# H3 convolution beside a SiLU feed-forward, on one core: where rows and signals are transposed, how the norm's root is made, and the list's DMA prices

## The chip, the core and the metric

One core of a Trainium2 chip. The metric is the device time of one execution in microseconds; of a set of runs the median counts. All traces are of the core's hardware profiler, one execution each.

## The reference

All inputs are float32; S = 2048 rows, D = 1024 channels, F = 3584.

```python
xn = layernorm(q)                       # per row, (x - m) / sqrt(v + 1e-5)
k_shift = causal_conv(k, shift_k)       # 4 taps per channel
kv = k_shift * v
y = irfft(rfft(kv, 2S) * rfft(ssm_k, 2S))[:S] + kv * ssm_D     # per channel
out = q + xn * y + silu(xn @ w1) @ w2
```

## The kernel before

**Number format.** Every product of float32 quantities runs as three float16 products: each factor is split into a high and a low part (`split`, line 363: one ScalarE activation for the high part, one VectorE instruction, line 345, for the rest), and high x high, high x low and low x high are accumulated. Lines 947 to 949 are those three products of the first feed-forward matmul, 1075 to 1077 of the second, 1506 to 1508 of the convolution's forward transform and 1697 to 1699 of its inverse.

**Feed-forward.** The first matmul treats its rows in two halves of 1024 (index `sp` 0 and 1), and within a half it uses a Strassen scheme with seven products (`PRODUCTS`): the factors of x are A11, A12, A21, A22 (upper and lower four row blocks, left and right half of the channels) and the sums S1 to S4 of them; the factors of w1 are B11 to B22 and T1 to T4. For the first half the x factors stay in SBUF in the places `x0` to `x7`. For the second half the sums are made row by row (`more_sums`), split and stored to DRAM (`xsp`), and read back by a transposing DMA (`load_x`, one DMA of 1 MB for each of seven factors) as soon as the first half's last use of a place is over.

**Norm and first factors, before.** `load_row` loads a row block (128 rows) as `xt`. `ln_rows` takes statistics on VectorE (`bn_stats`, line 493, two halves; `bn_aggr`, then two small copies, lines 498 and 499), in groups of 2, 2, 4 and 8 blocks; for each group ScalarE makes the square root, VectorE the reciprocal and one Newton step (lines 507 to 512), and VectorE normalizes each block in place (line 522). `ON_ACT` and `APPLY` name blocks whose statistics or normalization run on ScalarE; both are empty. `transposes` (line 539) turns the eight blocks of the first half with TensorE, each half block as four 128x128 float32 transposes into one of three PSUM tiles `ft`. From the transposed tiles the factors are split; `keep` copies the transposed upper blocks back over their rows with ScalarE, `lower_sums` copies A21 to `s` with ScalarE, and the sums S1 to S4 are made of transposed tiles on VectorE.

**The convolution.** Eight channel groups of 128 (index g). `gate` makes `acc` (the shifted k times v) with rows on partitions of its own order; `signal_parts` scales and splits it into `cm` (one buffer, `CMB` = 1), and two transposing DMAs, issued by SP (`X`, line 335), bring the high and low parts to `hi` and `lo`; the filter's parts are split into the same tiles. `stage1` multiplies them with the DFT constants `cfw` into PSUM tiles `ps`: each of four tiles t of a group has two banks, each first with three products, then evacuated by ScalarE (`to_spec`: `diff`), then with three more, then evacuated again. `PSB` is the number of `ps` banks, 3, and `py`, for the norms and the inverse transform, has 4 - `PSB`. While the second feed-forward matmul runs, a `ps` or `py` tile may use a bank of the feed-forward's ring `ff` where more than one is free (`spare`). `forward`, `product` and `inverse` are VectorE work on `spec` and `tmp`.

**Order.** All this is recorded by generators (streams), and a list scheduler, `Order.run`, writes the instructions of all engines in one order. Each operation has an engine, a busy time, a delay and a margin; DMAs have bytes besides, which pass through one modelled pipe (`self.pipe`). The stream whose head can start first, less its bias, goes next. The engines' queues then run in this order as they stand, so a price that is off shows as a wait at the head of a queue. Prices of DMAs: `L` for plain ones from SP (0.4 us busy), `X` for transposing ones (0.6 us busy, 1.2 times the bytes), `G` for accumulating ones from GpSimd (bytes as they are). The pipe is

```python
self.pipe = max(self.pipe, t + 3.0) + op.nbytes / 330e3
```

A table load is priced where an activation's function (Sqrt or Silu) is not the last one that was loaded.

Of the kernel before, what the change touches and what calls it, by code (L numbers as in the profile page):

```python
# [11 lines left out]
F32 = mybir.dt.float32  # L12
BF16 = mybir.dt.bfloat16
F16 = mybir.dt.float16
I32 = mybir.dt.int32
# [22 lines left out]
PSB = 3  # L38
XGB = 4
CMB = 1  # L40
ON_ACT = ()
APPLY = ()
# [69 lines left out]
class Order:  # L112
# [58 lines left out]
    def run(self):  # L171
        while self.streams:
# [122 lines left out]
def h3_ffn_kernel(ctx, tc, x, kp, vs, fs, shift, dskip, w1, w2, cfwd, cinv, out):  # L295
# [36 lines left out]
    def X(o, i, m=0.3):  # L332

        n = size(o) * o.shape[0] * mybir.dt.size(o.dtype)
        return Op("SP", 0.6, 0.1, lambda: nc.sync.dma_start(o, i, transpose=True), [i], [o], m, 1.2 * n)
# [12 lines left out]
    def a_act(o, i, func, scale=1.0, bias=None, total=None):  # L348
# [7 lines left out]
        p.table = func if func in (AF.Sqrt, AF.Silu) else None  # L356
# [23 lines left out]
    mean = cst.tile([P, NT], F32, name="mean")  # L380
# [38 lines left out]
    sums_r = s1_r = xst_r = Halves(order, lnp, "s", 6)  # L419
# [48 lines left out]
    def load_row(t):  # L468
        yield xts_r.ready
        xts[t] = xns[t] = xts_r.tile([P, D], uses=6 if t < 4 else 2)  # L470
# [3 lines left out]
    def ln_rows():  # L474
        for t0, n, bias in ((0, 2, 0.26), (2, 2, 0.17), (4, 4, 0.15), (8, 8, 0.03)):
            yield bias
            q = slice(t0, t0 + n)
            mv = lnp.tile([P, 6, 8], F32, name="mv", bufs=2)
            m = mv[:, :, 0:n]
            order_in = (8, 9, 12, 13, 10, 11, 14, 15) if n == 8 else range(t0, t0 + n)  # L480
            for n_, t in enumerate(order_in):
                yield flag["xt", t]
                xt, i = xts[t][0], slice(t - t0, t - t0 + 1)
                if t in ON_ACT:
                    yield a_act(wide, xt, AF.Copy, total=m[:, 1, i])
                    yield a_act(m[:, 0, i], m[:, 1, i], AF.Copy, -1.0 / D)
                    yield a_act(wide, xt, AF.Square, 1.0, m[:, 0, i], total=m[:, 1, i])
                    yield a_act(m[:, 3, i], m[:, 1, i], AF.Copy, 1.0 / D)
                    continue
                st = lnp.tile([P, 2, 6], F32, name="st", bufs=2)  # L490
                ag = lnp.tile([P, 2], F32, name="ag", bufs=2)
                for a in range(2):
                    yield V(lambda: nc.vector.bn_stats(st[:, a, :], xt[:, a * W:(a + 1) * W]), st[:, a, :],
                            [xt[:, a * W:(a + 1) * W]], us=0.65)

                def moments():
                    nc.vector.bn_aggr(ag, st)
                    nc.vector.tensor_scalar(m[:, 0, i], ag[:, 0:1], -1.0, None, op0=MUL)
                    nc.vector.tensor_copy(m[:, 3, i], ag[:, 1:2])
                p = V(moments, m[:, 0, i], [st], us=0.5)  # L500
                p.writes.append(m[:, 3, i])
                yield p
            yield V(lambda: nc.vector.tensor_scalar(m[:, 3, :], m[:, 3, :], 1e-5, None, op0=ADD), m[:, 3, :], [m[:, 3, :]], us=0.15)
            yield a_act(m[:, 4, :], m[:, 3, :], AF.Sqrt)

            def chain(m=m, q=q):
                nc.vector.reciprocal(m[:, 4, :], m[:, 4, :])
                nc.vector.tensor_mul(m[:, 5, :], m[:, 4, :], m[:, 4, :])
                nc.vector.tensor_mul(m[:, 5, :], m[:, 5, :], m[:, 3, :])
                nc.vector.tensor_scalar(m[:, 5, :], m[:, 5, :], -0.5, 1.5, op0=MUL, op1=ADD)  # L510
                nc.vector.tensor_mul(rstd[:, q], m[:, 4, :], m[:, 5, :])
                nc.vector.tensor_mul(nmr[:, q], m[:, 0, :], rstd[:, q])
            p = V(chain, rstd[:, q], [m[:, 3, :], m[:, 4, :], m[:, 0, :]], us=1.05)
            p.writes += [nmr[:, q], m[:, 5, :]]
            yield p
            for t in order_in:
                xt, i = xts[t][0], slice(t - t0, t - t0 + 1)
                if t in APPLY:
# [3 lines left out]
                yield V(lambda: nc.vector.tensor_scalar(xt, xt, m[:, 0, i], rstd[:, t:t + 1], op0=ADD, op1=MUL),  # L522
                        xt, [xt, m[:, 0, i], rstd[:, t:t + 1]], us=0.78)
                flag["xn", t].set()

    pts = []

    def transposes():
        jobs = [(t, a) for t in range(4) for a in range(2)]
        jobs += [(4 + i, a) for i in range(4) for a in range(2)]  # L530
        for t, a in jobs:
            yield flag["xn", t]
            xn, tok = xns[t]
            yield ft.ready
            pt, ptok = ft.tile([P, KH, P], uses=2)

            def mm():
                for c in range(KH):
                    nc.tensor.transpose(pt[:, c, :], xn[:, (KH * a + c) * P:(KH * a + c + 1) * P], ident)
            yield T(mm, pt, [xn], 0.5, m=0.3)  # L540
            tok.set()
            pts.append((pt, ptok))

    def next_pt():
        return bool(pts)

    def first_rows():
        for n, name in enumerate(("A11", "A12")):
            xo[0][name], xtok[0][name] = places[XPLACE[name]].tile([P, 4, KH, 2, P], F16)
        for t in range(4):  # L550
# [1275 lines left out]
```

## Time and profile before

| | before |
|---|---|
| median of 3 runs | 1296.15 us (1293.06 to 1300.64) |
| profiled execution, device time | 1294.81 us |
| its span in the trace | 1293.0 us |
| mean granted TensorE clock | 0.987 |
| busy: TensorE, VectorE, ScalarE, GpSimd | 1235.7, 1147.6, 727.0, 133.1 us |
| DMA moved | 289.25 MB, mean 224 GB/s |

The device time of the profiled execution holds 1.8 us besides the span. TensorE's busy time counts each matmul with its latency, so that neighbours overlap; its pace is read from the starts. In rows of groups, the columns are line, engine, operation, output and inputs by the program's names, shapes and count, then busy us and mean ns of one, then idle us just before them and what ended it. Stages are read as windows of the span.

### The profile page before, as it was taken

The page shows a single profiled execution, that of the slowest core. Times are in us where ns is not written, and L with a number is a line of the kernel's source. Part 1 is how long each engine was busy: PE and PEld are TensorE (multiplying, and loading weights), DVE is VectorE, ACT ScalarE, POOL GpSimd, SP SyncE. Part 2 cuts the span into 40 slices and gives each one's busy share as a digit, 9 for nine tenths or more (in the row PEclk, how much of TensorE's full clock was granted, in tenths as well). Part 3 has the DMA queues.
Part 4 walks back from the last instruction along what each step waited for, and adds up shares of the span by engine and source line. Part 5 has one row for each costly group of instructions (what it writes and reads, how often), then busy time and mean ns, then how long its engine had stood idle before and what let it go on. Part 6 is the DMA issues. An engine that isn't in the chain of part 4 may idle for free.

```text
span 1293.0 us, 16973 instructions
## 1 busy us (share of the span) xinstructions
PE 1235.7 (96%) x5954; PEld 590.2 (46%) x5954; DVE 1147.6 (89%) x1525; ACT 727.0 (56%) x1153; POOL 133.1 (10%) x141
## 2 busy tenths in 40 slices
PE   6899999998999999988999999999989999999997
PEld 6444444443444454434544444444444454444453
DVE  7999998896569989989998989999999989999961
ACT  6857886775676688656754442454173263542321
POOL 0000000000000020000310120120030030123241
PEclk9899999999999999999999999999999999999999
DMA  9447888899899999879997597599587597979785
GB/s 325 153 157 228 288 302 299 290 262 226 215 352 337 322 282 352 254 197 269 259 318 163 99 243 163 94 241 304 136 168 195 131 186 211 253 145 151 159 144 77
DMA packets 281364, 289.25 MB, mean 224 GB/s; under 512 B 78400, under 2 KB 197184, under 8 KB 280000
## 3 DMA queue, kind: packets, MB, share of 16 engines
q1 hardware_dynamic: 254544, 263.27, 67.5%
q0 software_dynamic: 26736, 24.92, 15.4%
q8 instruction: 46, 0.75, 0.3%
q14 instruction: 38, 0.31, 0.1%
HBM read 184.05 MB, written 96.73 MB: 217 GB/s over the span
## 4 chain that ended last, share of the span: by engine, by line
PE 35%; DVE 29%; DMA 16%; issue 12%; ACT 4%; POOL 2%; SPq 1%; POOLq 0%; ACTq 0%; DVEq 0%
DVE spec L342 8%; PE ff L948 6%; PE ff L947 6%; PE ff L949 6%; PE ff L1075 4%; PE ff L1077 4%; PE ff L1076 4%; DVE tmp L342 3%; DMA wraw<-in_w 3%; DMA lo<-cm 3%; DVE x L345 2%; POOL out L339 2%; DVE ht L345 2%; DVE wo L345 2%; DVE acc L345 2%
## 5 line engine op out<-in xcount | busy, mean ns | idle before, releaser
L1075 PE MATMUL ff<-x,wo 128*128 128x512 f16 x864 | 327.4, 379 | 5.1 <-DMA hi<-in_vs 2.7
L1077 PE MATMUL ff<-x,wo 128*128 128x512 f16 x864 | 327.4, 379 | 0.0
L1076 PE MATMUL ff<-x,wo 128*128 128x512 f16 x864 | 327.4, 379 | 0.0
L947 PE MATMUL ff<-x,wo 128*128 128x512 f16 (+1 forms) x808 | 306.2, 379 | 14.7 <-ACT hf L353 5.8
L948 PE MATMUL ff<-x,wo 128*128 128x512 f16 (+1 forms) x808 | 306.2, 379 | 2.6 <-DVE x L345 2.6
L949 PE MATMUL ff<-x,wo 128*128 128x512 f16 (+1 forms) x808 | 306.4, 379 | 1.8 <-DVE wo L345 1.8
L342 DVE TENSOR_TENSOR spec<-spec 128x512 f32<-128x512 f32 (+2 forms) x256 | 261.0, 1052 | 2.2
L1076 PEld LDWEIGHTS <-wo 128*128 128x128 f16 x864 | 84.5, 98 | 104.4 <-issue 6.2
L1077 PEld LDWEIGHTS <-wo 128*128 128x128 f16 x864 | 84.5, 98 | 102.0
L1075 PEld LDWEIGHTS <-wo 128*128 128x128 f16 x864 | 85.4, 99 | 98.6
L948 PEld LDWEIGHTS <-wo 128*128 128x128 f16 x808 | 79.8, 99 | 105.7 <-issue 18.5
L949 PEld LDWEIGHTS <-wo 128*128 128x128 f16 x808 | 79.7, 99 | 99.8 <-issue 6.4
L947 PEld LDWEIGHTS <-wo 128*128 128x128 f16 x808 | 81.4, 101 | 93.8 <-issue 3.0
L353 ACT ACTIVATE hf<-ff,invc 128x512 f32<-128x512 f32 x64 | 43.5, 680 | 102.6 <-PE ff L1077 93.0
L339 POOL DMA_DIRECT2D out<-hf x63 | 55.8, 886 | 437.9 <-ACT hf L353 390.5
L342 DVE TENSOR_TENSOR tmp<-spec 128x2048 f32<-128x2048 f32 (+1 forms) x48 | 92.1, 1932 | 0.7
L345 DVE SCALAR_TENSOR_TENSOR ht<-hf,wsc,ht 128x1024 f16<-128x1024 f32 (+1 forms) x56 | 67.3, 1203 | 18.0 <-ACT ht L353 17.9
L339 POOL DMA_DIRECT2D out<-xg x40 | 45.2, 1284 | 300.2 <-DMA lo<-cm 136.3
L345 DVE SCALAR_TENSOR_TENSOR wo<-raw,wsc,wo 128x512 f16<-128x512 f32 (+1 forms) x56 | 55.9, 1012 | 17.1 <-ACT wo L353 17.1
L353 ACT ACTIVATE ht<-hf,wsc 128x1024 f16<-128x1024 f32 (+1 forms) x56 | 60.7, 1085 | 15.5 <-DMA hs<-ht 5.0
L345 DVE SCALAR_TENSOR_TENSOR acc<-kin,taps,acc 128x1024 f32<-128x1024 f32 x48 | 61.4, 1278 | 8.8 <-ACT acc L353 8.8
L353 ACT ACTIVATE spec<-spec 128x1024 bf16<-128x1024 f32 x32 | 33.7, 1052 | 51.6 <-DVE spec L342 51.6
(178 smaller groups left out, 1747.5 us busy)
## 6 DMA issues: line engine op xcount, KB each, us to landing
wo<-hs SPq DMA_DIRECT2D x160, 256.0 KB, 3.7
hs<-ht SPq DMA_DIRECT2D x80, 256.0 KB, 5.6
out<-hf POOLq DMA_DIRECT2D x63, 256.0 KB, 4.4
raw<-in_w SPq DMA_DIRECT2D x28, 512.0 KB, 5.6
wraw<-in_w SPq DMA_DIRECT2D x24, 512.0 KB, 6.6
w2n<-in_w SPq DMA_DIRECT2D x24, 512.0 KB, 6.6
kin<-in_kp SPq DMA_DIRECT2D x16, 704.0 KB, 5.4
xt<-in_x SPq DMA_DIRECT2D x16, 512.0 KB, 7.3
```

The costliest lines, as they stand in the source:

```text
L339: return Op("POOL", 1.1, 3.0, lambda: nc.gpsimd.dma_start(o, i, accum_op=ADD), [i], [o], m, n)
L342: return V(lambda: nc.vector.tensor_tensor(o, a, b, op=op), o, [a, b], **k)
L345: return V(lambda: nc.vector.scalar_tensor_tensor(o, a, s, b, op0=op0, op1=op1), o, [a, b] + ([] if isinstance(s, float) else [s]), **k)
L353: nc.scalar.activation(o, i, func, scale=scale, **kw)
L947: nc.tensor.matmul(o, w[:, 0, k], xf[:, :, k, 0], start=first and k == 0, stop=False, **kw)
L948: nc.tensor.matmul(o, w[:, 0, k], xf[:, :, k, 1], start=False, stop=False, **kw)
L949: nc.tensor.matmul(o, w[:, 1, k], xf[:, :, k, 0], start=False, stop=last and k == KH - 1, **kw)
L1075: nc.tensor.matmul(po, hx[:, n, 0, :], wc[:, n, 0, :], start=first and n == 0, stop=False, **kw)
L1076: nc.tensor.matmul(po, hx[:, n, 0, :], wc[:, n, 1, :], start=False, stop=False, **kw)
L1077: nc.tensor.matmul(po, hx[:, n, 1, :], wc[:, n, 0, :], start=False, stop=last and n == 3, **kw)
```

## The change

- **Row sums row-major.** The sums S1 to S4 of the first half are made of normalized rows in place (`xt`), and then transposed as the rows were: 128 transposes of 128x128 at that line instead of 64. `keep`, `lower_sums`, `upper_sums` and the copies to `xt` and `s` are gone. The bias of the stream of sums is 0.13 instead of 0.03, that of the transposes 0.1 instead of 0.03.
- **Norm.** 1/sqrt(v + eps) is made on VectorE alone, from a first guess by shifting the bits, one step of third order and one Newton step (11 small instructions). Blocks 4 and 5 have their statistics, blocks 4 to 7 their normalization on ScalarE. Sqrt is not used any more, and the Silu table is loaded at the start.
- **Signal parts.** Groups 0 to 2 transpose `acc` with TensorE into a `py` bank (four 128x128 float32 transposes for each tile), and the splits read PSUM. Groups 3 to 7 go by `cm` and DMA as before. `PSB` is 2: two `ps` and two `py` banks.
- **Prices.** The pipe, `X` and `G` as in the diff.
- **Copies and squares.** The second eight of the sixteen copies of x to the output, which earlier followed the units of the second half, wait for the first finished tile of the second matmul; the loads for the squares of w2 wait for unit 1 of the second half.

```diff
-PSB = 3
+PSB = 2
+BY_DMA = 3
-ON_ACT = ()
-APPLY = ()
+EPS = 1e-5
+SQ = 1
+LB = 0.15
+ON_ACT = (4, 5)
+APPLY = (4, 5, 6, 7)
+GUESS = 0x5f3759df
...
-        self.table = None
+        self.table = AF.Silu
...
-                self.pipe = max(self.pipe, t + 3.0) + op.nbytes / 330e3
+                self.pipe = max(self.pipe, t + op.busy + 2.4) + op.nbytes / 345e3
...
     def X(o, i, m=0.3):
         n = size(o) * o.shape[0] * mybir.dt.size(o.dtype)
-        return Op("SP", 0.6, 0.1, lambda: nc.sync.dma_start(o, i, transpose=True), [i], [o], m, 1.2 * n)
+        k = 1.2 if i.space == bass.MemoryType.DRAM else 3.0
+        return Op("SP", 0.65 + n / 240e3, 0.1, lambda: nc.sync.dma_start(o, i, transpose=True), [i], [o], m, k * n)
     def G(o, i, m=0.3):
-        return Op("POOL", 1.1, 3.0, lambda: nc.gpsimd.dma_start(o, i, accum_op=ADD), [i], [o], m, n)
+        return Op("POOL", 1.1, 3.0, lambda: nc.gpsimd.dma_start(o, i, accum_op=ADD), [i], [o], m, 2.3 * n)
...
+            def chain():
+                tt, ts, stt = nc.vector.tensor_tensor, nc.vector.tensor_scalar, nc.vector.scalar_tensor_tensor
+                ts(v, var, EPS, None, op0=ADD)
+                ts(r.bitcast(I32), v.bitcast(I32), 1, 0, op0=ALU.logical_shift_right, op1=ALU.logical_shift_left)
+                ts(r.bitcast(I32), r.bitcast(I32), -1, GUESS, op0=MUL, op1=ADD)
+                tt(e, v, r, op=MUL)
+                tt(e, e, r, op=MUL)
+                ts(f, e, 0.375, -1.25, op0=MUL, op1=ADD)
+                tt(e, e, f, op=MUL)
+                stt(r, e, 1.875, r, op0=ADD, op1=MUL)
+                tt(e, v, r, op=MUL)
+                stt(e, e, -0.5, r, op0=MUL, op1=MUL)
+                stt(r, e, 1.5, r, op0=ADD, op1=MUL)
...
+    def turned(src, tok, name, i, bias):
+        yield ft.ready
+        pt, ptok = ft.tile([P, KH, P])
+        def mm():
+            for c in range(KH):
+                nc.tensor.transpose(pt[:, c, :], src[:, c * P:(c + 1) * P], ident)
+        yield T(mm, pt, [src], 0.44, m=0.3)
+        ...
+        add(split(o[:, :, 0], o[:, :, 1], pt, XS, after), bias)
...
     def x_rows():
+        for i in range(4):
+            for name in ("A21", "A22"):
+                yield flag["turned", name, i]
+            x, z = xns[i][0], xns[4 + i][0]
+            yield v_tt(z[:, W:], z[:, 0:W], z[:, W:], ADD)
+            flag["summed", "S1", i].set()
+            yield v_tt(z[:, 0:W], x[:, 0:W], z[:, 0:W], SUB)
+            flag["summed", "S3", i].set()
+        for i in range(4):
+            x, z = xns[i][0], xns[4 + i][0]
+            yield v_tt(x[:, 0:W], z[:, W:], x[:, 0:W], SUB)
+            flag["summed", "S2", i].set()
+            yield v_tt(x[:, W:], x[:, W:], x[:, 0:W], SUB)
+            flag["summed", "S4", i].set()
...
     def copies():
         for a in range(NT):
-            yield flag["unit", a // 2]
+            yield flag["unit", a // 2] if a < NT // 2 else flag["half"]
...
     def squares_w2():
         yield lambda: "wraw" in ctxs
+        yield flag["unit", SQ]
...
         def signal_parts():
...
                 for t in TO:
+                    if g < BY_DMA:
+                        yield py_r.ready
+                        px, ptok = py_r.tile([P, 2, 2, P])
+                        def mm():
+                            for b in range(2):
+                                for i in range(2):
+                                    nc.tensor.transpose(px[:, b, i, :], acc[:, b, t + 4 * i, :], ident)
+                        yield T(mm, px, [acc[:, :, t::4, :]], 0.44, m=2.0)
+                        (hi, htok), (lo, ltok) = part[g, t] = yield from parts_tile(hi_r, lo_r)
+                        flag["part", g, t].n = 2
+                        add(split(hi[:, 0], lo[:, 0], px, sc[:, 0:1], (ptok, flag["part", g, t])), CB)
+                        add(split(hi[:, 1], lo[:, 1], kf[:, :, t::4, :], sc[:, 1:2], (ktok, flag["part", g, t])), CB)
+                        continue
                     yield cm_r.ready
...
-    nc.scalar.activation(warm, ones[:, 0:1], AF.Sqrt)
+    nc.scalar.activation(warm, ones[:, 0:1], AF.Silu)
-    add(x_rows(), 0.03)
+    add(x_rows(), 0.13)
-    add(transposes(), 0.03)
+    add(transposes(), 0.1)
```

More of the change, by code (lines that the diff above doesn't have):

```diff
@@ L504, in ln_rows @@
[L504 to L512, printed above, removed]
@@ L513, in ln_rows @@
[L513 to L514 removed]
+                yield V(lambda: nc.vector.bn_aggr(ag[:, t - t0], st), ag[:, t - t0], [st], us=0.2)
+            q = slice(t0, t0 + n)
+            mean, var, r = ag[:, 0:n, 0], ag[:, 0:n, 1], rstd[:, q]
+            e, f, v = (nt[:, k, 0:n] for k in range(3))
+            def chain():
[11 more added lines that the diff above has]
+                stt(r, e, 1.5, r, op0=ADD, op1=MUL)
@@ L521, in ln_rows @@
                     continue
-                yield V(lambda: nc.vector.tensor_scalar(xt, xt, m[:, 0, i], rstd[:, t:t + 1], op0=ADD, op1=MUL),
-                        xt, [xt, m[:, 0, i], rstd[:, t:t + 1]], us=0.78)
+                yield V(lambda: nc.vector.tensor_scalar(xt, xt, ag[:, t - t0, 0:1], rstd[:, t:t + 1], op0=SUB, op1=MUL),
+                        xt, [xt, ag[:, t - t0], rstd[:, t:t + 1]], us=0.78)
                 flag["xn", t].set()
-    pts = []
-    def transposes():
[L529 to L542, printed above, removed]
```

152 lines of the change are left out of this document (44 added, 108 removed).

## The prediction

> **What bounds the kernel now.** I read the page's head and its costliest groups first, then the windows of single stages, then TensorE's own line of time. The page:
>
> ```profile
> span 1293.0 us, 16973 instructions
> ...
> PE 1235.7 (96%) x5954; PEld 590.2 (46%) x5954; DVE 1147.6 (89%) x1525; ACT 727.0 (56%) x1153; POOL 133.1 (10%) x141
> ...
> L1075 PE MATMUL ff<-x,wo 128*128 128x512 f16 x864 | 327.4, 379 | 5.1 <-DMA hi<-in_vs 2.7
> ...
> L947 PE MATMUL ff<-x,wo 128*128 128x512 f16 (+1 forms) x808 | 306.2, 379 | 14.7 <-ACT hf L353 5.8
> ```
>
> The busy share of 96% is no proof, since 379 ns is one matmul's latency. The pace is read from starts that follow each other; the columns are start, length, engine and line:
>
> ```profile
> 76.16 0.38 PE L949 MATMUL ff<-x,wo 128*128 128x512 f16 x1
> 76.37 0.38 PE L947 MATMUL ff<-x,wo 128*128 128x512 f16 x1
> ...
> 60.04 0.63 PE L947 MATMUL ff<-x,wo 128*128 128x512 f16 x1
> 60.47 0.63 PE L948 MATMUL ff<-x,wo 128*128 128x512 f16 x1
> ...
> 24.11 1.51 PE L539 MATMUL ft<-ident,xt 128*128 128x128 f32 x12
> ```
>
> A product of 512 columns costs 0.216 us at full clock (76.16 to 76.37, rounded) and 0.43 us at half clock (60.04 to 60.47). Twelve float32 transposes cost 1.51 us, of which the last one's latency is about 0.3, so one costs 0.11 us. Lines 947 to 949 and 1075 to 1077 hold 3 x 808 + 3 x 864 = 5016 products, at 0.216 us about 1083 us of the span, before the convolution's products. TensorE therefore is the bound, and a microsecond counts only if it is TensorE's work, its idle time, or its clock. The stages (length; then busy us of PE, PEld, DVE, ACT and POOL; then granted clock, DMA share and GB/s) show the three:
>
> ```profile
> 51.40:61.60 10.20, 7.14 (x22) 3.74 (x23) 9.89 (x17) 7.38 (x14) 0.00 (x0) 0.50 0.69 237
> 300.00:400.00 100.00, 93.91 (x410) 41.10 (x409) 65.00 (x71) 61.68 (x100) 0.76 (x1) 0.95 1.01 279
> 314.00:317.60 3.60, 3.60 (x11) 1.31 (x9) 0.26 (x1) 1.44 (x2) 0.00 (x0) 0.53 1.01 203
> 321.00:324.60 3.60, 3.60 (x11) 1.28 (x10) 1.41 (x2) 1.43 (x3) 0.00 (x0) 0.53 0.66 128
> 338.00:341.40 3.40, 3.37 (x9) 1.20 (x9) 2.65 (x5) 2.98 (x5) 0.00 (x0) 0.52 0.62 174
> 1210.00:1240.00 30.00, 30.00 (x143) 13.76 (x141) 29.48 (x38) 9.65 (x14) 4.83 (x6) 1.00 0.75 159
> ```
>
> 1210 to 1240 is a stage without loss. 300 to 400 is one where the DMA engines are full (1.01) and VectorE works only 65 of 100 us; there TensorE idles and drops to half clock three times. TensorE's waits, summed over the run (us, times, longest):
>
> ```profile
> PE ps L1506 <- ACT tmp L353: 6.4, 3, 2.6
> PE ff L947 <- ACT hf L353: 5.8, 4, 3.3
> PE ft L539 <- ACT xt L353: 5.8, 2, 3.8
> PE ff L947 <- DVE hf L342: 3.5, 2, 2.2
> PE ft L539 <- DVE x L345: 3.3, 3, 1.5
> PE ff L1075 <- DMA hi<-in_vs: 2.7, 1, 2.7
> PE ff L948 <- DVE x L345: 2.6, 3, 1.5
> ```
>
> **The change, part by part.** The sum is made against the profiled execution, 1294.81 us (its span and 1.8 us around it); the three runs' median, 1296.15, lies 1.3 us above that, inside their own scatter of 7.6, and I make no correction for it.
>
> *Transposes added: +12.3 us.* Making the sums in row-major order takes rows through TensorE after the sums as well: 128 transposes at line 539 instead of 64. Groups 0 to 2 of the convolution get 3 x 4 x 4 = 48 more. At 0.11 us these are 7.0 and 5.3 us, and they lie on the bound engine.
>
> *The opening: -10 us besides its transposes.* The rows of its other engines:
>
> ```profile
> L345 DVE SCALAR_TENSOR_TENSOR ht<-hf,wsc,ht 128x1024 f16<-128x1024 f32 (+1 forms) x56 | 67.3, 1203 | 18.0 <-ACT ht L353 17.9
> ...
> L353 ACT ACTIVATE junk<-raw 128x1024 bf16<-128x1024 f32 x24 | 25.1, 1046 | 0.2
> ...
> L522 DVE TENSOR_SCALAR xt<-xt,mv,rstd 128x1024 f32<-128x1024 f32 x16 | 12.2, 807 | 0.0
> ...
> L493 DVE BATCH_NORM_STATS2 st<-xt 128x6 f32<-128x512 f32 x32 | 21.2, 683 | 3.6 <-DMA xt<-in_x 3.6
> ...
> L345 DVE SCALAR_TENSOR_TENSOR x<-ft,x 128x512 f16<-128x512 f32 x16 | 10.6, 685 | 1.2 <-ACT xt L353 0.9 <-ACT x L353 0.2
> ...
> L342 DVE TENSOR_TENSOR xt<-xt 128x512 f32<-128x512 f32 x8 | 5.5, 688 | 0.1
> ...
> L353 ACT ACTIVATE xt<-ft 128x512 f32<-128x512 f32 x8 | 4.7, 608 | 0.6 <-DVE x L345 0.6
> ...
> L353 ACT ACT_TABLE_LOAD x5 | 6.4, 1283 | 0.1
> ...
> 8.13 0.17 DVE L503 TENSOR_SCALAR mv<-mv 128x2 f32<-128x2 f32 x1
> ...
> 9.90 0.16 DVE L511 TENSOR_TENSOR rstd<-mv 128x2 f32<-128x2 f32 x1
> 10.10 0.16 DVE L512 TENSOR_TENSOR nmr<-mv,rstd 128x2 f32<-128x2 f32 x1
> 10.18 1.53 DVE L522 TENSOR_SCALAR xt<-xt,mv,rstd 128x1024 f32<-128x1024 f32 x2
> ```
>
> Lost there today: the two waits on ACT xt (5.8; these copies back to rows are removed), the waits on DVE x (3.3 and 2.6), and half of 7.14 us at half clock in 51.4 to 61.6 (3.6), together 15.3 us. VectorE sets the later ones, and it gets lighter: two rows' statistics go to ScalarE (4 x 0.68 = 2.7 us), four normalizations too (4 x 0.81 = 3.2), and with the small copies at L498 and L499 some 7 us before the lower rows can be transposed. The bit chain is not a gain in itself: 11 dependent small instructions at 0.20 us (the starts at 9.90 and 10.10) are 2.2 us, where today's chain with its ScalarE square root takes from 8.13 to 10.18. ScalarE loses the table loads that return to the square root (all but one load of 1.28 us) and 12 copies of 0.6 us, and gains four normalizations and four passes over rows at the 1.05 us of a junk row; it works 7.4 of the 10.2 us of the first window, which hides the rest. What remains to wait for comes from the order in which the changed program's instructions stand: from the first to the last transpose of the lower rows and sums VectorE has 24 splits x 0.66 (10.6/16) + 16 sums x 0.69 + about 9 us of weights and stores (512 columns at 0.69, 1024 at 1.2), some 36 us in all, less about 0.07 us per instruction where they overlap (807 ns each at L522, yet 1.53 for two), 33; TensorE has 96 x 0.11 + 93 x 0.216 = 31 us in the same stretch. So it waits 2 to 3 us there and about 3 before its first products, whose path hardly changes: 5 of the 15.3 remain. I take -10; the ends are -15 (nothing remains) and +3 (VectorE's 36 us in full, and ScalarE's normalizations late).
>
> *The turn to the second half of the rows, and the transposes by DMA: -14 us.* TensorE's line there, the SP queue's row for the reloads (min/median/max ns), and one later stall, with ScalarE's row that caused it:
>
> ```profile
> 313.64 0.38 PE L947 MATMUL ff<-x,wo 128*128 128x512 f16 x1 [2.04 <-DMA x<-xspA]
> ...
> 320.08 0.39 PE L947 MATMUL ff<-x,wo 128*128 128x512 f16 x1 [2.00 <-DMA x<-xspS]
> ...
> 337.55 0.38 PE L1506 MATMUL ps<-hi,cfw 128*128 128x512 f16 x1 [1.95 <-DMA hi<-cm]
> ...
> L335 SPq DMA_TRANSPOSE x<-xspS x4: 4625/5491/6774, 290.4 to 320.7; - x4
> ...
> 555.03 0.72 ACT L353 ACTIVATE cm<-acc,csc 128x512 f16<-128x512 f32 x1 [4.90 <-DMA lo<-cm]
> ...
> 556.29 0.38 PE L947 MATMUL ff<-x,wo 128*128 128x512 f16 x1 [3.28 <-ACT hf L353]
> ```
>
> Three waits are 6.0 us, and the three half-clock windows behind them cost half of 10.6, 5.3. The stall at 556 is ScalarE blocked 4.9 us for the one buffer cm; TensorE waits 3.28 for the evacuation queued behind it. Together 14.6 us, and a half-clock window behind 556 of the same length as the others would add 1.7: 16.3. A reload holds SP 5.5 us, while the list priced it at 0.6, so seven of them throw SP 30 us behind and everything queued there with them. The new price (0.65 + n/240e3, n of 1 MB: 5.0 us) agrees with the row. In the changed order three plain DMAs stand among the reloads instead of ten and two transposes of cm, and group 0's products, now fed through TensorE, stand between the products that need reloaded factors. The reloads still need 7 x 5.5 = 38 us of SP, so I leave 2 us of waiting and take -14; ends -16 and 0.
>
> *Two ps banks instead of three: +2 us.* The nearest row is the wait on ACT tmp, 6.4 us in 3 times, 2.1 each: it could go, or double. I take one more such wait; ends -6 and +6.
>
> *Re-priced list elsewhere: 0.* New prices shift the order everywhere. The waits on ACT hf, DVE hf and hi<-in_vs left after the above (5.8 - 3.3 + 3.5 + 2.7) are 9 us, and can vanish or double. The last eight copies of x to out move behind the first finished output tile, and the squares of w2 behind a unit; both only lighten 300 to 400, where the DMA share is 1.01, and the later stage that takes them stands at 0.75 in 1210 to 1240, which hides them.
>
> Sum: 1294.8 + 12.3 - 10 - 14 + 2 = 1285.1 us.
>
> **Rivals.** *The waits shrink further:* the more accurate prices also close the 9 us and the ACT tmp waits; for it speaks that most follow a DMA which came later than listed. 1285 - 9 - 6 = 1270.
>
> *A wait takes the place of the one removed:* the reloads still come too late, and the opening stays bound by VectorE. Half of 14 stays, and the opening gives 7 instead of 10: 1285 + 7 + 3 = 1295. For it: SP's 38 us of reloads are untouched.
>
> *Slower by the ps banks:* in the changed order groups 0 to 2 stand as three products into a bank, three to nine of the feed-forward, and again three into the same bank, which must wait for ScalarE's copy. There are 32 tiles; if every third pays 2.1 us, 11 x 2.1 = 23, and 1308 comes out. It beats the gain from five such waits on and passes +0.5% at nine. Against it: today's group 1 stands as close, and no row of the waits names it.
>
> *Slower by the clock:* the stretch 51.4 to 61.6 at 0.50 began when TensorE had only transposes and waits behind it. With twice the transposes mixed into the products, the whole stretch of 31 us could run at half clock: +31 less what is waiting anyway, about 1315. It decides if windows that hold more products than transposes still count as idle; in the changed order no more than 12 transposes (1.5 us) follow each other in that stretch, which speaks against it. The Trainium skill, "TensorE: Matmul & The Clock Gate", Part 4, says that transposes do not count as activity for the clock in the way matmuls do; by that rule this rival gains, and the 0.50 in the first window agrees with it.
>
> That the change does not do what it says is excluded by the instruction counts: 128 and 48 transposes, 40 instead of 64 transposes of cm by DMA.
>
> **How the numbers follow.** About 0.5% (6.5 us) is what a measurement of this kernel can tell from no change: 1289.7 and 1302.6. Forecast 0.54, its own range 1275 to 1296 from the ends above taken against each other, three quarters of it below 1289.7; further shrinking 0.14; the wait that stays 0.13, mostly within 0.5%; ps banks 0.12; clock 0.07. Faster 0.40 + 0.14 + 0.03 = 0.57; same 0.13 + 0.09 = 0.22; slower 0.12 + 0.07 + 0.02 = 0.21. The range 1266 to 1306 leaves out the clock, the upper half of the ps banks and a few per cent below.
>
> **What would show it.** Right: no wait of line 539's successor on ACT xt; TensorE at full clock from about 25 us on; no half-clock windows at the reloads and at most 2 us of waits on x<-xsp; no ACT cm wait before group 3; transposes of acc at 0.11 us. Wrong: waits of ps on ACT tmp or spec in more than six places; a granted clock of 0.5 between 35 and 75 us; new waits on ACT hf of the sum of those removed.

## The result, and the profile after

| | before | after |
|---|---|---|
| median | 1294.61 us (1290.58 to 1300.64, 4 runs) | 1259.22 us (1257.32 to 1261.67, 4 runs) |
| profiled execution, device time | 1294.81 us | 1259.29 us |
| its span | 1293.0 us | 1257.5 us |
| mean granted TensorE clock | 0.987 | 0.996 |

The ratio is 0.9724, 95% interval 0.9681 to 0.9767: faster by 35 us, where 10 were forecast, and below the range's low end of 1266.

From the page of the kernel after, its head, the clock in 40 slices, the two data queues (packets, MB, share of 16 engines' time) and the feed-forward's costliest groups:

```profile
span 1257.5 us, 17095 instructions
...
PE 1234.0 (98%) x6066; PEld 600.4 (48%) x6066; DVE 1137.8 (90%) x1503; ACT 724.8 (58%) x1148; POOL 132.8 (11%) x141
...
PEclk8999999999999999999999999999999999999999
...
q1 hardware_dynamic: 241488, 260.12, 66.8%
q0 software_dynamic: 26736, 24.92, 15.4%
...
L1016 PE MATMUL ff<-x,wo 128*128 128x512 f16 x864 | 327.4, 379 | 1.0 <-ACT hf L359 1.0
...
L887 PE MATMUL ff<-x,wo 128*128 128x512 f16 (+1 forms) x808 | 303.5, 376 | 3.9 <-ACT hf L359 2.6
```

TensorE has 112 instructions more and ends 35 us earlier, so what went is waiting and half clock. Idle time before the first feed-forward line (L947, now L887) fell from 14.7 to 3.9 us, before the second (L1075, now L1016) from 5.1 to 1.0. TensorE's waits in the kernel after (us in total, times, longest):

```profile
PE ft L547 <- DVE x L351: 3.8, 3, 2.1
PE ft L547 <- DVE xt L528: 2.8, 2, 2.4
PE ff L887 <- ACT hf L359: 2.6, 3, 1.4
PE ff L888 <- DVE x L351: 1.4, 2, 1.0
PE ps L1462 <- ACT tmp L359: 1.2, 2, 0.6
PE ff L887 <- DVE hf L348: 1.2, 1, 1.2
PE ft L1717 <- DVE one L398: 1.1, 1, 1.1
PE ff L1016 <- ACT hf L359: 1.0, 2, 0.8
PE ff L889 <- DVE wo L351: 0.2, 1, 0.2
```

No transfer is waited for any more, and ps <- ACT tmp, at the head of the list before with 6.4 us, is 1.2. The stages as windows (columns as in the prediction), first of the kernel before, then of the one after:

```profile
25.00:70.00 45.00, 35.94 (x191) 20.12 (x190) 43.25 (x96) 36.30 (x60) 0.00 (x0) 0.89 0.45 149
200.00:345.00 145.00, 135.33 (x604) 59.98 (x603) 111.68 (x162) 95.53 (x133) 0.95 (x1) 0.96 0.94 256
500.00:700.00 200.00, 190.29 (x902) 88.58 (x901) 187.78 (x225) 124.39 (x198) 14.07 (x14) 0.99 0.91 261
700.00:1000.00 300.00, 289.78 (x1415) 137.88 (x1414) 282.97 (x327) 128.13 (x226) 45.73 (x46) 1.00 0.75 180
```
```profile
25.00:70.00 45.00, 42.09 (x264) 27.16 (x265) 44.07 (x87) 34.80 (x58) 0.00 (x0) 1.00 0.28 92
200.00:345.00 145.00, 143.34 (x677) 66.50 (x676) 127.78 (x174) 105.74 (x151) 1.71 (x2) 1.00 0.90 254
500.00:700.00 200.00, 197.29 (x967) 94.69 (x965) 193.01 (x241) 120.37 (x182) 19.21 (x19) 1.00 0.88 255
700.00:1000.00 300.00, 299.30 (x1448) 141.65 (x1447) 279.28 (x324) 125.83 (x220) 42.04 (x44) 1.00 0.77 188
```

All four gained. TensorE's busy time rose by 8.0 us at the turn and by 7.0 and 9.5 in the last two stages. The 7.0 hold the stall at 556 of the kernel before, which the prediction booked with the turn, and the last transposes of `acc` (1.8 us up to 569). The 9.5 lie where, of all the edits, only the prices, the bank count and the moved copies still act.

For a finer account I took the distance of each TensorE start to the next one, less the pace of what was started (0.216 us per 512 columns, 0.11 per transpose, twice that in half-clock windows); the rest is waiting. Work at pace within the half-clock windows is their cost. In us:

| | before | after | difference | prediction |
|---|---|---|---|---|
| work at pace | 1218.1 | 1230.4 | +12.3 | +12.3 |
| opening, 0 to 70: waits + half clock | 20.2 + 5.0 | 12.1 + 2.2 | -10.9 | -10 |
| turn, 200 to 345, and the stall at 556 | 11.4 + 5.1, 3.4 + 1.7 | 2.1, 0 | -19.5 | -14 |
| rest behind 345 | 23.6 | 6.1 | -17.5 | +2 (ps banks), 0 (list) |
| sum | | | -35.6 | -10 |

The last matmul starts 35.3 us earlier (1284.4 to 1249.1). Before there were 58.5 us of waits and 11.9 of half clock, 70 us in all; after, 20.4 and 2.2.

### The profile page after: what moved, and what is told of

Its sections match the earlier page's. It is cut to its first block, busy times and chain, and to the rows that moved or that the text cites. A ratio compares the mean times of both kernels' runs of the same rounds, so it can differ in the third digit from the quotient of the medians.

```text
span 1257.5 us, 17095 instructions
## 1 busy us (share of the span) xinstructions
PE 1234.0 (98%) x6066; PEld 600.4 (48%) x6066; DVE 1137.8 (90%) x1503; ACT 724.8 (58%) x1148; POOL 132.8 (11%) x141
## 3 DMA queue, kind: packets, MB, share of 16 engines
q1 hardware_dynamic: 241488, 260.12, 66.8%
q0 software_dynamic: 26736, 24.92, 15.4%
## 5 line engine op out<-in xcount | busy, mean ns | idle before, releaser
L1016 PE MATMUL ff<-x,wo 128*128 128x512 f16 x864 | 327.4, 379 | 1.0 <-ACT hf L359 1.0
L887 PE MATMUL ff<-x,wo 128*128 128x512 f16 (+1 forms) x808 | 303.5, 376 | 3.9 <-ACT hf L359 2.6
L1016 PEld LDWEIGHTS <-wo 128*128 128x128 f16 x864 | 85.5, 99 | 98.8
L887 PEld LDWEIGHTS <-wo 128*128 128x128 f16 x808 | 80.8, 100 | 86.9
L359 ACT ACTIVATE spec<-ps 128x512 f32<-128x512 f32 x84 | 48.7, 591 | 36.8 <-PE ps L1464 35.9
L359 ACT ACTIVATE wo<-raw,wsc 128x512 f16<-128x512 f32 (+1 forms) x56 | 51.6, 927 | 27.6 <-DVE raw L348 14.8
```

The lines of the kernel that those rows point to most:

```text
L359: nc.scalar.activation(o, i, func, scale=scale, **kw)
L887: nc.tensor.matmul(o, w[:, 0, k], xf[:, :, k, 0], start=first and k == 0, stop=False, **kw)
L1016: nc.tensor.matmul(po, hx[:, n, 0, :], wc[:, n, 0, :], start=first and n == 0, stop=False, **kw)
```

## The experiments

Line numbers in kernels that differ by a line are shifted by one. "Ratio" is to the kernel before, run on the same chip (its median lay between 1292.0 and 1294.6 in every set), with the 95% interval.

**Parts of the change alone.** e1 is the changed kernel with the three old prices; e2 the kernel before with the three new ones and nothing else:

```diff
-                self.pipe = max(self.pipe, t + 3.0) + op.nbytes / 330e3
+                self.pipe = max(self.pipe, t + op.busy + 2.4) + op.nbytes / 345e3
...
-        return Op("SP", 0.6, 0.1, ..., m, 1.2 * n)                  # X
+        k = 1.2 if i.space == bass.MemoryType.DRAM else 3.0
+        return Op("SP", 0.65 + n / 240e3, 0.1, ..., m, k * n)
...
-        return Op("POOL", 1.1, 3.0, ..., m, n)                      # G
+        return Op("POOL", 1.1, 3.0, ..., m, 2.3 * n)
```

> The changed kernel with the three old DMA prices in the list (pipe, X, G), all else as changed. Theory 1, the prices took the waits away all over the run: the median returns by two thirds of the gain, to about 1283 us, with waits of TensorE on ACT hf, on x<-xsp and a half-clock window at the reloads back. Theory 2, the parts gain by themselves (transposes of groups 0 to 2 off the DMA queue, lighter opening): at most 1268 us, the opening unchanged at full clock from 20 us on. Theory 3, any new order moves the waits by chance: anything within 1250 to 1275, with waits in new places.

> The kernel before with the three new DMA prices alone. Theory 1: about 1272 us, no half-clock window at the reloads (314 to 341 us) and no ACT cm stall before TensorE at 556; the opening with its half-clock window of 10 us stays. Theory 2: within 6 us of 1294.6, since the transposes of cm are still on SP's queue and the opening is the old one. Theory 3: 1280 to 1310.

e3 is the kernel before with the transposes of groups 0 to 2 by TensorE, and so with two ps banks; e4 the kernel before with the new opening (norm, row sums, biases):

```diff
-PSB = 3
+PSB = 2
+BY_DMA = 3        # and the branch in signal_parts
```

> The kernel before, with groups 0 to 2 transposed by TensorE and two ps banks, nothing else. Theory 2: 1294.6 + 5.3 for 48 transposes - 10 for the waits on hi<-cm and behind ACT cm with their half-clock windows, about 1290. Theory 1: no gain without prices, 1295 to 1302, the waits on x<-xsp stay. Theory 3: 1280 to 1310.

> The kernel before with the new opening alone: row sums row-major with 64 more transposes, norm's root by bits, ScalarE's share of the norm, the new biases of these streams. As predicted: 1294.6 - 3, about 1292, no half-clock window at 51 to 62 us, waits from 311 us on as before. Theory 2 with a larger opening than predicted: 1280 to 1285, TensorE's line past 75 us earlier by 10 us or more. Theory 1: 1290 or more.

| | median us | ratio |
|---|---|---|
| e1 after, old prices | 1276.0 | 0.9883 [0.9858, 0.9908] |
| e2 before, new prices | 1282.96 | 0.9935 [0.9914, 0.9956] |
| e3 before, transposes of groups 0 to 2 by TensorE | 1284.08 | 0.9938 [0.9917, 0.9959] |
| e4 before, new opening | 1285.55 | 0.9949 [0.9929, 0.9970] |

e1 loses 17 us of the 35, so the prices, booked at 0 outside opening and turn, are the largest single part. But e2, e3 and e4 each gain 6 to 9, and that needs a control: every edit makes the list write another order.

**Orders shaken without meaning.** The pipe's 330e3 (or 345e3) is changed by 3e3, under 1%:

```diff
-                self.pipe = max(self.pipe, t + 3.0) + op.nbytes / 330e3
+                self.pipe = max(self.pipe, t + 3.0) + op.nbytes / 327e3      # e6, e11; 333e3 in e15
...
-                self.pipe = max(self.pipe, t + op.busy + 2.4) + op.nbytes / 345e3
+                self.pipe = max(self.pipe, t + op.busy + 2.4) + op.nbytes / 342e3   # e5; 348e3 in e18
```

> The changed kernel with the pipe's rate at 342e3 instead of 345e3 bytes per us, a change of 0.9% in one price that means nothing. If the gain comes from causes (accurate prices, fewer DMA transposes, a lighter opening): within 4 us of 1259. If the changed list is one lucky order among many (theory 3): 1265 to 1280, with the small waits in other places.

> The kernel before with the pipe's rate at 327e3 instead of 330e3. Causes: within 5 us of its own median of 1292. Theory 3, the order before was an unlucky one: 1275 to 1288, and then some of what the single parts gained (6 to 9 us each) is the shake and not the part.

> The changed kernel with the three old prices, the pipe at 327e3 instead of 330e3. If old prices cost the changed kernel 17 us by cause: 1270 to 1282 again, with the wait at 280 us. If the 17 us were one unlucky order: 1259 to 1266.

> The kernel before with 333e3 instead of 330e3 in the pipe, a second change without meaning (327e3 gave 0.9925). If the kernel before is one order out of a scatter of some 10 us, and an unlucky one: 1280 to 1295. If lower prices of the pipe were better as such, 333e3 would be slower than before by as much as 327e3 was faster: 1300 to 1306.

> The changed kernel with 348e3 instead of 345e3 in the pipe, a change without meaning (342e3 gave 1262.3). If the new prices make a neighbourhood of good orders: 1257 to 1266. If the changed kernel is one lucky order of a scatter as wide as that of the kernel before: 1266 to 1280.

| | median us | ratio |
|---|---|---|
| e6 before, 327e3 | 1285.31 | 0.9925 [0.9907, 0.9943] |
| e15 before, 333e3 | 1296.75 | 1.0017 [0.9999, 1.0035] |
| e11 after, old prices, 327e3 | 1286.35 | 0.9927 [0.9899, 0.9954] |
| e5 after, 342e3 | 1262.32 | 0.9752 [0.9735, 0.9768] |
| e18 after, 348e3 | 1267.69 | 0.9801 [0.9764, 0.9838] |

A nudge without meaning gives the kernel before 9 us. So the totals of e2, e3 and e4 tell nothing of their parts: what one order happens to give is as large as what each part gives alone. Nor do the expectations fare well: e18 falls just into the range set for a lucky order, and e11, like e16 below, is slower than any of its theories allowed. I take means over such neighbours: before 1294.6, 1285.3 and 1296.8, mean 1292.2; after 1259.2, 1262.3 and 1267.7, mean 1263.1; after with old prices 1276.0 and 1286.4, mean 1281.2. By these the other parts bring 11 us under the old prices and the prices another 18 on top; the remaining 6 of the 35 are a good draw on one side and a poor one on the other. The groups with new and with old prices do not overlap (1259 to 1268 against 1276 to 1286). The changed kernel with old prices and the kernel before do, by a microsecond, so that the 11 are not shown by the totals. With two or three members each, the sizes are good to some 6 us. In the kernel before, the new prices (e2, 1283) gave no more than the nudge of e6 (1285).

The finer account by stage separates more than the totals do. Waits and half clock in the profiled executions, in us (behind 345 with the stall at 556):

| | opening, 0 to 70 | turn, 200 to 345 | behind 345 |
|---|---|---|---|
| before, e6, e15 | 25, 26, 26 | 17, 17, 16 | 29, 17, 32 |
| e1, e11 (changed, old prices) | 18, 15 | 8, 5 | 12, 27 |
| after, e5, e18 | 14, 14, 14 | 2, 2, 2 | 6, 13, 12 |

Opening and turn hardly move under a nudge, and what they gained is clear of the scatter. In all 20 profiled kernels the opening loses 25 to 27 us in its old form and 14 to 18 in the new one, whatever the prices. Behind 345 one order differs from the next by up to 15 us. There the three kernels before lose 26 on average and the three changed ones 10, but e1 with old prices loses no more than e5 and e18 with new ones.

**The prices one by one**, each in the changed kernel: e9 with X as before, e13 with G, e14 with the pipe, e10 with both of the latter, and e16 with a pipe that lands every transfer still later:

```diff
-                self.pipe = max(self.pipe, t + op.busy + 2.4) + op.nbytes / 345e3
+                self.pipe = max(self.pipe, t + op.busy + 3.4) + op.nbytes / 300e3     # e16
```

> The changed kernel with the old price of transposing DMAs (SP busy 0.6 us, 1.2 times the bytes) and the new pipe and G. If it is the reloads' 5.5 us of SP, listed at 0.6, that the list must know: 1270 or more, a long wait of TensorE at 280 to 330 us with half clock behind it. If the other two prices carry the gain: within 4 us of 1259. By chance of the order alone: 1259 to 1266, as the nudged run.

> The changed kernel with the new price of transposing DMAs alone; pipe and G old. If the reloads' price is the cause: 1259 to 1264. If the accumulating DMAs' bytes (listed at 1.0, now 2.3 times) and the pipe matter from 600 us on: 1268 or more, with waits of TensorE on ACT tmp and ACT hf behind 700 us.

> The changed kernel with the accumulating DMAs priced at their bytes as before, the other two new prices kept. Earlier runs: with all three prices old 1276.0 and 1286.4, with the new X alone 1279.6, without the new X 1270.4, with all three 1259 to 1266. Theory A, the pipe carries most of the gain and G little: 1259 to 1266. Theory B, G carries it (the accumulating queue took 2.4 times the engines' time per byte of the other one): 1270 to 1280. Theory C, any departure from the three together brings the old scatter back: 1268 to 1286 here and with the old pipe alike.

> The changed kernel with the pipe as before (start at t + 3.0 whatever the engine's hold, 330e3 bytes per us), new X and G kept. Theory A, the pipe carries most of the gain: 1270 to 1280. Theory B, G carries it: 1259 to 1266. Theory C, all three are needed: 1268 to 1286.

> The changed kernel with a pipe that is listed slower still (start 3.4 us after the engine is free instead of 2.4, 300e3 bytes per us instead of 345e3), so that every DMA lands later in the list than now. If the gain comes from loads not being listed too early: 1255 to 1262. If the present price is about right and a later one only makes the list wait for what has landed already: 1262 to 1275.

| | median us | ratio | waits + half clock, 200 to 345 | the same behind 500 |
|---|---|---|---|---|
| after | 1259.22 | 0.9724 [0.9681, 0.9767] | 2.1 | 5.8 |
| e9 old X | 1270.43 | 0.9814 [0.9790, 0.9837] | 9.8 | 10.8 |
| e13 old G | 1272.04 | 0.9835 [0.9808, 0.9861] | 2.1 | 18.3 |
| e14 old pipe | 1268.83 | 0.9798 [0.9773, 0.9823] | 12.2 | 5.5 |
| e10 old pipe and G | 1279.58 | 0.9879 [0.9853, 0.9904] | 9.5 | 15.8 |
| e16 slower pipe | 1277.38 | 0.9867 [0.9848, 0.9887] | 9.2 | 18.4 |

Each old price costs 10 to 13 us against the changed kernel, 6 to 9 against the mean of its neighbours; the two together cost more. All six kernels with an old price (1269 to 1286) are slower than all seven with the three new ones (1259 to 1268; e7, e8, e12 and e17 below included). That the prices matter is thereby shown, but not each one alone: e14 lies only 1.1 us above the nudge e18, and by the ratio not above it at all. Theory C, all three are needed, fits, but is not shown. Where the loss comes back differs: without the new pipe at the turn, without the new G behind 500, without both (e10) in both places, without the new X mostly at the turn. The nudged e5 and e18 stay at 2 us at the turn, yet e5 loses 13 us behind 500, so that the 18 of e13 are only 5 more than an edit without meaning lost. And e11, with all three old prices, loses only 5 at the turn, less than e9 or e14 with one: how much an old price costs there hangs on the order too. The turn in e9, then in e14:

```profile
200.00:345.00 145.00, 138.90 (x642) 63.83 (x641) 117.41 (x165) 104.02 (x148) 1.71 (x2) 0.98 0.88 249
```
```profile
200.00:345.00 145.00, 137.40 (x633) 63.14 (x631) 117.66 (x171) 101.62 (x145) 1.71 (x2) 0.96 0.89 248
```

Without the new G the turn is whole and the second matmul's stage is not (e13, windows and its longest wait):

```profile
200.00:345.00 145.00, 143.41 (x677) 66.55 (x676) 127.89 (x174) 106.11 (x151) 1.72 (x2) 1.00 0.90 254
500.00:700.00 200.00, 194.22 (x939) 92.12 (x938) 191.13 (x233) 118.75 (x179) 18.52 (x19) 0.99 0.85 248
700.00:1000.00 300.00, 295.86 (x1432) 140.00 (x1430) 273.54 (x321) 121.16 (x214) 41.92 (x43) 1.00 0.75 186
```
```profile
PE ps L1462 <- ACT tmp L359: 5.8, 3, 2.1
```

That is the wait which headed the list of the kernel before. ScalarE's line of time shows how it arises in e13, and how in the kernel before:

```profile
899.97 2.19 ACT L359 ACTIVATE zh<-spec,csc 128x1024 f16<-128x1024 f32 x2 [10.80 <-DVE spec L351]
902.06 1.06 ACT L359 ACTIVATE tmp<-ps 128x512 f32<-128x512 f32 x2
```
```profile
936.81 2.19 ACT L353 ACTIVATE zh<-spec,csc 128x1024 f16<-128x1024 f32 x2 [11.44 <-DVE spec L345]
938.90 1.06 ACT L353 ACTIVATE tmp<-ps 128x512 f32<-128x512 f32 x2
```

ScalarE stands 11 us at the head of its queue for VectorE's spec; the two evacuations of ps are queued behind it, and TensorE's next product into ps has been put too early in its own order. The bank count does not explain it: e13 has the same two banks as the kernel after. In the kernel after ScalarE stands there as long,

```profile
896.93 1.15 ACT L359 ACTIVATE zh<-spec,csc 128x1024 f16<-128x1024 f32 x1 [13.03 <-DVE spec L351]
```

but TensorE has feed-forward products in its order to fill that time, and its list of waits shows no more than 1.2 us for ps on ACT tmp. Two more runs bear on the banks. e3, the kernel before with two ps banks, waits as long as the kernel before with three (6.2 us against 6.4):

```profile
PE ps L1525 <- ACT tmp L358: 6.2, 3, 2.7
```

And this wait does not follow G alone: it is 2.2 us in e10, which has the old G, and 3.1 in the nudged e5, which has all new prices.

e16 refutes the simple form of my theory, that loads were listed too early. Listed later still, ScalarE's waits for transfers do shrink further (summed over their rows: 137.5 us before, 100.3 after, 40.8 in e16), yet 18 us are lost against the kernel after (14 against the mean of its neighbours). TensorE's longest waits in e16:

```profile
PE ff L887 <- DVE hf L348: 8.8, 1, 8.8
PE ff L889 <- DVE wo L351: 4.4, 6, 1.8
PE ff L887 <- ACT wo L359: 3.8, 4, 1.3
```

TensorE now waits for VectorE, and for weights that ScalarE and VectorE split. That the list takes weights and inputs for late and puts VectorE's other work ahead of them fits this, but was not followed instruction by instruction. So a price can be off in both directions, and ScalarE's waits for transfers are no measure of the gain. On an idle pipe a plain transfer of 256 KB is listed to land after 0.4 + 2.4 + 0.76 + 0.2 = 3.8 us in the kernel after, 4.0 before, 4.9 in e16; the page of the kernel after (KB each, median us to landing) has

```profile
wo<-hs SPq DMA_DIRECT2D x160, 256.0 KB, 4.0
```

and that of the kernel before 3.7. For a plain transfer, then, the old and the new price are both near. For a reload the new one is further off. On an idle pipe the list lets it land after 5.0 + 2.4 + 3.6 + 0.2 = 11.3 us (3.0 + 3.8 + 0.2 = 7.0 by the three old prices), while the list of transfers of the kernel after, under a busy pipe, has

```profile
x<-xspS SPq DMA_TRANSPOSE x4, 7.8
```

So what came closer to the trace is how long a reload holds SP and how much an accumulating transfer takes of the pipe, not when a transfer lands. Why the pipe's present price does better than the old one is not shown.

**The other parts, each taken out of the changed kernel.** e7: old copies and squares. e8: all groups by `cm` and DMA, and three ps banks. e12: old opening. e17: one more group by TensorE.

```diff
-            yield flag["unit", a // 2] if a < NT // 2 else flag["half"]
+            yield flag["unit", a // 2]          # e7, and no wait of squares_w2
...
-PSB = 2
-BY_DMA = 3
+PSB = 3                                     # e8, without the branch in signal_parts
...
-BY_DMA = 3
+BY_DMA = 4                                  # e17
```

> The changed kernel with the sixteen copies and the squares of w2 as before (no wait for the first output tile, none for unit 1). Causes as predicted: within 3 us of 1259, the DMA share at 300 to 400 us higher. If the DMA engines' load at 300 to 600 us is the missing part between the three single gains (24 us) and the whole (33 us): 1268 or more, with waits of TensorE between 280 and 600 us.

> The changed kernel with all groups transposed by DMA and three ps banks, as before. 48 transposes less are 5.3 us less of TensorE's work. Theory of causes: the waits behind cm in groups 0 to 2 come back in part, since the prices now know of them; 1259 - 5 + 10 to 14, about 1266. If the prices alone were enough to order round the DMA transposes: 1254. Theory 3: anything to 1280.

> The changed kernel with the old opening (sums of transposed tiles, square root on ScalarE, old biases); new prices, groups 0 to 2 by TensorE, new copies. As predicted for the opening: 1259 + 3 = 1262, the half-clock window at 51 to 62 us back, the rest as changed. If the lighter opening also helps later: 1268 or more.

> The changed kernel with one more group's signal transposed by TensorE (groups 0 to 3, DMA from group 4 on): 16 more transposes at 0.11 us, 1.8 us of work, and 8 fewer transposes by DMA. Group 3 lies behind the reloads of x. If what the transposes of groups 0 to 2 bring is only the room they make at the reloads: 1260 to 1266, no gain. If the wait of ScalarE for the buffer cm (11.6 us in 6 times in the changed kernel) still costs anything: 1254 to 1258.

| | median us | ratio |
|---|---|---|
| e7 old copies and squares | 1260.95 | 0.9737 [0.9722, 0.9752] |
| e8 all groups by DMA | 1266.45 | 0.9788 [0.9768, 0.9808] |
| e12 old opening | 1265.62 | 0.9777 [0.9754, 0.9801] |
| e17 DMA from group 4 on | 1263.05 | 0.9755 [0.9716, 0.9794] |

e7 and e17 are within the scatter: the copies and squares are worth nothing that shows, as forecast, and a fourth group by TensorE gives nothing back for its 1.8 us of work. e8 and e12 are 6 to 7 us slower than the kernel after, no more than e18 is; that their parts matter rests on the place. e12's opening is that of the kernel before, and e8's turn loses again (first e12, then e8):

```profile
25.00:70.00 45.00, 35.17 (x186) 19.27 (x185) 43.22 (x96) 36.40 (x60) 0.00 (x0) 0.89 0.46 150
```
```profile
200.00:345.00 145.00, 137.19 (x629) 61.91 (x628) 113.00 (x161) 98.78 (x140) 0.95 (x1) 0.98 0.90 256
```

e8 holds the new prices, and still waits 8.6 us at the turn against 2.1, with 2.4 of half clock besides. Over the 20 profiled kernels, the six without transposes by TensorE lose 11 to 17 us there, the seven with them and an old price 2 to 12, e16 with its slower pipe 9, and the six with them and the new prices 2 to 5. So at the turn the transposes by TensorE were needed, and the prices in most orders (e13, with the old G, loses only 2). No experiment beat the changed kernel.

## Why the prediction was wrong

**Transposes, +12.3: right.** Work at pace rose by 12.3, but that is only 112 more transposes times the pace put in. What confirms the pace are the starts: the twelve transposes from 38.54 on are followed by a product at 39.85, and four of `acc` from 287.74 on by one at 288.18, 0.11 us each. The rows of the two transposing lines of the kernel after:

```profile
L547 PE MATMUL ft<-ident,xt 128*128 128x128 f32 x128 | 17.9, 280 | 6.5 <-DVE x L351 3.8 <-DVE xt L528 2.8
...
L1415 PE MATMUL py<-ident,acc 128*128 128x128 f32 x48 | 7.2, 273 | 0.0
```

**Opening, -10: right.** -10.9 in the account above; the 384th product of the feed-forward starts 3.6 us earlier, transposes paid, where the sum said 3. The wait on ACT xt is gone and the full clock came, as the prediction's last part wanted. I expected 5 us to remain, 12.1 of waits do, but there were more before (20.2) than the rows I added up. That the new opening makes this gain is shown by the 20 kernels above, whatever their prices.

**The rival "slower by the clock": did not happen.** The window 12.20 to 19.00 of the kernel after is at half clock, and behind it none until the tail. Its row, and that of line 547 alone in the stretch the rival spoke of:

```profile
12.20:19.00 6.80, 4.50 (x22) 2.98 (x21) 6.63 (x17) 6.66 (x16) 0.00 (x0) 0.50 1.05 398
```
```profile
35.00:75.00 40.00, 12.94 (x96) 11.00 (x96) 1.00 0.31 111
```

All 96 transposes of the lower rows and sums ran between 35 and 75 us at a granted clock of 1.00, mixed with products. The Trainium skill, "TensorE: Matmul & The Clock Gate", Part 4, says that transposes do not count as activity in the way matmuls do. Mixed with products as here, that cost nothing; whether it holds for transposes alone no run here shows.

**The turn, -14: right in kind, 5.5 short.** In the kernel after, SP's rows for the reloads and for cm, and ScalarE's wait for cm:

```profile
L341 SPq DMA_TRANSPOSE hi<-cm x20: 1189/1202/1687, 646.8 to 1127.4; - x20
L341 SPq DMA_TRANSPOSE lo<-cm x20: 1188/1248/3121, 648.2 to 1129.3; - x20
L341 SPq DMA_TRANSPOSE x<-xspS x4: 4882/5071/6202, 283.3 to 305.1; - x4
L341 SPq DMA_TRANSPOSE x<-xspA x3: 4891/5470/5494, 275.5 to 310.2; - x3
```
```profile
ACT cm L359 <- DMA lo<-cm: 11.6, 6, 3.3
```

The seven reloads still hold SP for 37 us (four at 5.07, three at 5.47), but TensorE waits for none: the list now prices one at 5.0 us and starts them earlier, those of xspS from 283.3 to 305.1 instead of from 290.4 to 320.7 (to 312.1 in e9 with the old X, to 315.6 in e14 with the old pipe). I had left 2 us of waits on x<-xsp; there are none. This sign is weaker than I took it for: e2, e3 and e6 show no such wait either, and lose 16, 7 and 17 us at the turn all the same. The rest is smaller waits of this stage, which I had not counted, because I took the three long ones only.

**Ps banks, +2: wrong in sign.** I booked one more wait of ps on ACT tmp; 6.4 us fell to 1.2. e13 and e3 show that the order makes these waits and not the number of banks: two banks have 1.2 us of them in the one order, 5.8 and 6.2 in the others. The rival "slower by the ps banks" did not happen.

**Re-priced list elsewhere, 0: this is the step that failed.** With the ps waits, the stages behind 345 gave 17.5 us, where the prediction had 0 and +2. The whole stretch behind 345, the stall at 556 included, gave 22.6 us in this pair and 15 on the average of the nudged neighbours. The cause is only in part shown: old prices in the changed kernel lose 12 and 27 there against 6 to 13 with new ones, so some of the 17.5 us may be the draw of the order. I had written that "new prices shift the order everywhere" and that the waits left "can vanish or double", and took the middle. Two mistakes lie in it. First, the new prices are not a coin toss: old prices in the changed kernel gave 1276 and 1286, new ones 1259 to 1268. I had used the evidence for that myself, at the turn only: the new hold of SP agreed with the reloads' row. Two more agree: 128 KB from cm is now listed at 0.65 + 131072/240e3 = 1.20 us, and its rows say 1.20 and 1.25. In the page's queue rows 24.92 MB of accumulating transfers take 15.4% of the engines' time and 260.12 MB of the others 66.8%, per MB 0.618 against 0.257, a factor 2.4, where G now says 2.3. Secondly, I counted 9 us to be had there, and 6 for the ps banks, where 24 lay. A row of the waits counts from the end of the last product's latency of 0.38 us, while the next one could start after 0.22, so each stop costs 0.16 more than its row says (3.28 in the row of 556.29, 3.44 by the starts), and many small rows add up. The rival "the waits shrink further" had the right mechanism, at 0.14 and 15 us; by the account above it was worth 19.5 behind 345, and the turn gave 5.5 more.

**Range.** The low end of 1266 followed from that count. TensorE's total loss of 70 us was to be had from the trace of before, and a floor at 1295 + 12 - 70 = 1237 would have held the result. Some of the miss is the draw: the nudged neighbours of the kernel after are 3 and 8 us slower, and e18, at 1267.7, lies within the range.

One slip of the prediction changes nothing: its 1083 us count all 5016 products at 512 columns, but 96 of them have 256, which takes 10 us off.

What stays open: how much each price is worth alone, since the differences (6 to 13 us) are close to the scatter of single orders (9 us); how much of the gain behind 345 is the prices and how much the draw; and whether G's factor belongs to the accumulation or to the queue it runs in.

## What to carry to other kernels

Where a list of estimated prices writes the order, compare each changed price with the durations in the trace, and do not book the new order at nothing: here three new prices, two of which had moved towards the trace, were worth some 18 us in the changed kernel, and a pipe listed slower still lost most of it. The bound engine's total loss between its starts bounds what can be gained. Before reading a gain of under 1% from one part, shake the order by an edit without meaning and see how far the time moves. When a part's total is no larger than that scatter, look at the stage where its loss comes back, and at the same stage of the shaken orders beside it.

## What the runs showed that I had not expected

An edit of under 1% in one price moved the time by 9 us (1294.6 to 1285.3). The accumulating queue took 2.4 times the engines' time per byte of the other queue. Two transposes of 128 KB from SBUF hold SP 2.45 us between them, half as long as one of 1 MB from DRAM (5.1 to 5.5), and so nearly twice as long per byte; whether the size or the source makes that, no run here separates.

Nor does the length of a wait alone decide whether half clock follows. In the kernel before, a wait of 1.95 us (337.55, in the prediction's rows) was followed by 3.4 us at 0.52, and a longer one by none; its row in TensorE's line of time, and the window behind it:

```profile
939.53 0.38 PE L1506 MATMUL ps<-hi,cfw 128*128 128x512 f16 x1 [2.58 <-ACT tmp L353]
```
```profile
939.00:943.00 4.00, 3.47 (x23) 2.15 (x23) 3.72 (x5) 3.28 (x7) 0.00 (x0) 1.00 0.20 36
```

So the sum's "half of 3.4 us behind each stall" is no rule.
